# A retention and mixture-of-attention kernel: normalisation ahead of the projections, another order of the start, zero rows under the last tile

## The chip, the cores and the metric

The kernel runs on one core of one Trainium2 chip. Time is device microseconds (us) of one launch. The engines are PE (matmuls; its weight loads are shown apart as PEld), DVE, ACT and POOL (vector work) and SP, which issues the DMAs. Each works through its own instructions in the order in which the program wrote them, and waits on semaphores for the others.

## The reference

Two layers follow one another, for 8 batches, 8 heads, 576 positions and 64 channels per head, all in float32:

```python
# 1: retention, per head with its own decay gamma
scores = scale * (q @ k.T)
ret = scores * where(rel >= 0, gamma ** rel, 0)       # rel = row - column
x = concat over heads of (ret @ v)                    # [B, 576, 512]
# 2: four attention experts of width 64, two chosen per row
logits = x @ w_gate                                   # the two largest of 4, softmax -> w
for e in range(4):
    q, k, v = x @ wq[e], x @ wk[e], x @ wv[e]
    a = softmax(where(causal, scale * q @ k.T, -1e9))
    out += w[e] * (a @ v @ wo[e])                     # w is 0 where e was not chosen
```

## The kernel before, in words

Rows go in tiles of 128, so a batch has five: four of 128 rows and a last one of 64 (the table CH). Tiles 0 and 1 form range 0 (256 rows), tiles 2 to 4 range 1 (320 rows). The program is one loop over n = 0 to 41 and an `end()`; iteration n works on retention tile n (batch n // 5, tile n % 5), finishes retention tile n - 1, takes attention tile n - 6 through scores and softmax, and attention tile n - 7 through transposes and the product with V. So every stage of five iterations repeats for each batch.

The names that the prediction uses, with their tiles:

- `load` brings x (q and k of a tile, transposed) and vk (v and k) through SP's queue. `decay` multiplies v by powers of gamma in place (vk, L102), on DVE for the first four tiles and on POOL from then on (`gp if n > 3 else v`).
- `qk` makes the 64 x 64 products of q and k (qk, L135), copies them out on ACT (p, L138), and POOL masks them (L141). `state` makes k-by-v products (st, L115) and adds them up on DVE (s, L121 and L123).
- `result` is a generator: in its first part q times the earlier state (old, L164), v times the masked products (own, L174), the copies and adds into x32 (x, L167 on ACT, L178 and L179 on DVE); after its first yield the multiply by a table (L184), the rounded high part xh (L185, ACT) and the rest xl (L186). L184 and L186 are on DVE for the first two tiles and on POOL later.
- `proj` (pj, L225) makes attention's q and k, `vproj` (pv, L249) its v and the gate's logits. Each sums three products, high by high, high by low and low by high, since xh, xl and the weights wh, wl are in a reduced float format. `vproj` copies the logits out on DVE (lg, L254 and L256). `weights` splits a weight into high (ACT, L210) and low (DVE, L211).
- `scores` (ss, L315 or L324 for the 64-row tile) with its softmax steps: masked row minimum on DVE (L334, L338), exponential with its sum on ACT (L342). `normal` divides by the sum and multiplies by the gate: three small DVE instructions (L354 to L361) and one pass over each expert's probabilities (L363). `turn` transposes them on PE (pt, L378) and copies the result out on DVE or ACT (L381, L383). `values` multiplies by V (ys, L400). `outproj` (po, L425) writes the result through ACT and SP.

All PE results go through eight PSUM banks of one tag: a new tile takes the bank of the eighth tile before it, and waits until that one's reader is done. Which projections an iteration runs stands in the table STEPS: of batch b, q and k of range 0 in iteration 5b+3, v of range 0 in 5b+5, q and k of range 1 in 5b+6, v of range 1 in 5b+7, output in 5b+9 and 5b+12; batch 0 has its own places. The order of PE, DVE, ACT and POOL is the order of these calls, since the program is scheduled by hand; SP's order is set by the compiler. Within an iteration it is: retention of tile n (`qk`, `state`) interleaved with `result(n - 1)`, `scores` of the new tile with `turn` of the old one between its softmax steps, the second part of `result`, `decay(n + 1)`, the gate, `weights`, the projections (`work(n)`), `normal` of the new tile, `values` of the old one.

In the 64-row tile all blocks are cut to 64 where a column block or a row block ends: `vproj` loads 64 columns, the fifth transpose is 128 x 64, and the fifth step of `values` contracts 64 rows.

## Time and profile before

| | |
|---|---|
| median of three runs | 484.05 us (483.19 to 485.59) |
| the profiled execution's own time | 484.3 us |
| its span | 482.6 us, 19026 instructions |
| granted TensorE clock, mean | 0.982 |
| moved by DMA | 50.98 MB, 106 GB/s in the mean |

A timeline row reads: start and length in us, engine, line, operation, what it writes from what it reads, shape, count, and in brackets idle time of the engine before it and what ended that. For PE the shape begins with rows times columns of the array that are in use (64\*64, 128\*64, 128\*128). Consecutive instructions of one line are merged, so a row's length goes from the first start to the last end; ends of matmuls are modelled, and the start of the next row is the better clock. A row of the wait list reads: who waited for whom, us in total, how often, the longest. A row of the groups by shape: count, busy us in total, mean ns of one, idle time before them.

### The profile page before, as it was taken

The page shows a single profiled execution, that of the slowest core. Times are in us where ns is not written, and L with a number is a line of the kernel's source. Part 1 is how long each engine was busy: PE and PEld are TensorE (multiplying, and loading weights), DVE is VectorE, ACT ScalarE, POOL GpSimd, SP SyncE. Part 2 cuts the span into 40 slices and gives each one's busy share as a digit, 9 for nine tenths or more (in the row PEclk, how much of TensorE's full clock was granted, in tenths as well). Part 3 has the DMA queues.
Part 4 walks back from the last instruction along what each step waited for, and adds up shares of the span by engine and source line. Part 5 has one row for each costly group of instructions (what it writes and reads, how often), then busy time and mean ns, then how long its engine had stood idle before and what let it go on. Part 6 is the DMA issues. An engine that isn't in the chain of part 4 may idle for free.

```text
span 482.6 us, 19026 instructions
## 1 busy us (share of the span) xinstructions
PE 458.3 (95%) x7996; PEld 401.6 (83%) x7996; DVE 314.0 (65%) x1135; ACT 260.0 (54%) x814; POOL 216.0 (45%) x276
## 2 busy tenths in 40 slices
PE   7597999999999999999999999999999999998996
PEld 4486978898789888899888997799788997877785
DVE  2832878663986648864787639866487737793662
ACT  2652667545565455745475455664476455654472
POOL 2247545544465435564355444654446543420100
PEclk8797999999999999999999999999999999999999
DMA  8943322314243142413423142522423110000021
GB/s 288 385 178 134 107 94 88 134 46 144 90 156 111 58 140 89 168 46 103 131 90 133 45 145 90 176 92 75 157 90 133 48 57 1 3 30 16 2 87 67
DMA packets 22516, 50.98 MB, mean 106 GB/s; under 512 B 2720, under 2 KB 11680, under 8 KB 22432
## 3 DMA queue, kind: packets, MB, share of 16 engines
q1 hardware_dynamic: 22432, 49.77, 29.8%
q8 instruction: 63, 1.03, 0.9%
q14 instruction: 21, 0.17, 0.1%
HBM read 40.33 MB, written 9.44 MB: 103 GB/s over the span
## 4 chain that ended last, share of the span: by engine, by line
PE 80%; DVE 9%; ACT 5%; issue 2%; DMA 2%; POOL 1%; SPq 0%; DVEq 0%; ACTq 0%; POOLq 0%
PE pj L225 21%; PE pv L249 11%; PE ys L400 10%; PE po L425 10%; PE pt L378 9%; PE ss L315 5%; PE qk L135 4%; DVE p L363 3%; PE ss L324 3%; PE own L174 2%; PE st L115 2%; PE old L164 2%; DVE x L179 2%; DMA gi<-gi 2%; ACT p L138 1%
## 5 line engine op out<-in xcount | busy, mean ns | idle before, releaser
L342 ACT ACTIVATE p<-p,nm 128x128 f32<-128x128 f32 (+4 forms) x144 | 83.0, 578 | 89.5 <-DVE nm L334 67.4
L186 POOL TENSOR_TENSOR xl<-x,xh 128x512 fp32r<-128x512 f32 (+1 forms) x38 | 44.6, 1174 | 97.3 <-ACT xh L185 97.3
L363 DVE TENSOR_SCALAR p<-p,sm 128x128 f32<-128x128 f32 (+4 forms) x144 | 70.7, 551 | 1.4
L414 POOL CAST yh<-y 128x256 fp32r<-128x256 f32 (+1 forms) x39 | 17.5, 449 | 112.2 <-ACT y L413 112.2
L378 PEld LDWEIGHTS pt<-con,p 128*128 128x128 f32 (+1 forms) x400 | 42.7, 139 | 28.7 <-issue 12.5
L141 POOL TENSOR_SCALAR_AFFINE_SELECT p<-p 64x512 f32<-64x512 f32 (+1 forms) x80 | 49.8, 623 | 30.0 <-ACT p L138 27.2
L334 DVE CUSTOM_DVE_ANT_0 p<-ss,mask 128x512 f32<-128x512 f32 (+3 forms) x128 | 56.2, 482 | 8.5 <-PE ss L315 8.5
L378 PE MATMUL pt<-con,p 128*128 128x128 f32 (+1 forms) x400 | 55.1, 280 | 7.0 <-DVE x L179 3.5
L400 PE MATMUL ys<-pth,vn 128*64 128x128 f32 (+2 forms) x960 | 56.6, 262 | 0.0
L400 PEld LDWEIGHTS ys<-pth,vn 128*64 128x64 f32 (+1 forms) x960 | 46.2, 136 | 8.1 <-issue 3.1
L184 POOL TENSOR_TENSOR x<-x,gi 128x512 f32<-128x512 f32 (+1 forms) x38 | 44.5, 1170 | 13.5 <-PE pt L378 8.7
L254 DVE COPY lg<-pv 128x4 f32<-128x4 f32 (+1 forms) x40 | 6.4, 160 | 66.3 <-ACT vn L253 66.2
L179 DVE TENSOR_TENSOR x<-x,own 128x256 f32<-128x256 f32 (+1 forms) x80 | 26.3, 361 | 35.0 <-ACT x L167 34.7
L315 PE MATMUL ss<-k,q 64*64 64x512 f32 (+3 forms) x512 | 42.6, 432 | 0.5 <-issue 0.5
L381 DVE COPY pth<-pt 128x512 f32<-128x512 f32 (+3 forms) x80 | 37.6, 483 | 4.5 <-PE pt L378 4.2
L102 POOL TENSOR_TENSOR vk<-vk,con 128x512 f32<-128x512 f32 (+1 forms) x36 | 35.3, 980 | 0.0
L383 ACT ACTIVATE pth<-pt 128x512 f32<-128x512 f32 (+3 forms) x80 | 33.1, 420 | 0.5 <-PE pt L378 0.4
L413 ACT ACTIVATE y<-ys 128x256 f32<-128x256 f32 (+1 forms) x39 | 14.1, 363 | 32.7 <-PE ys L400 32.3
L138 ACT ACTIVATE p<-qk 128x256 f32<-128x256 f32 (+1 forms) x80 | 24.6, 359 | 11.3 <-PE qk L135 11.3
L185 ACT ACTIVATE xh<-x 128x512 fp32r<-128x512 f32 (+1 forms) x40 | 23.2, 579 | 11.6 <-POOL x L184 8.0
L253 ACT ACTIVATE vn<-pv 128x256 f32<-128x256 f32 (+1 forms) x40 | 15.1, 381 | 26.5 <-PE pv L249 26.5
L425 PE MATMUL po<-yh,who 128*128 128x320 f32 (+1 forms) x128 | 28.8, 306 | 0.6 <-ACT yh L409 0.6
(89 smaller groups left out, 1038.6 us busy)
## 6 DMA issues: line engine op xcount, KB each, us to landing
x<-xf SPq DMA_DIRECT2D x32, 512.0 KB, 4.3
vk<-vkf SPq DMA_DIRECT2D x32, 512.0 KB, 5.3
out<-ot SPq DMA_DIRECT2D x32, 160.0 KB, 1.9
out<-ot SPq DMA_DIRECT2D x32, 128.0 KB, 1.8
raw<-wraw SPq DMA_DIRECT2D x4, 512.0 KB, 7.0
x<-xt SPq DMA_DIRECT2D x8, 256.0 KB, 2.6
vk<-vkt SPq DMA_DIRECT2D x8, 256.0 KB, 3.2
gi<-gi SPq DMA_DIRECT2D x1, 256.0 KB, 7.6
```

Source lines behind the costliest of these rows:

```text
L141: gp.affine_select(w, w, pattern=[[0, 4 * k], [1, 64]], base=0, channel_multiplier=-1, compare_op=OP.is_ge, fill=0.0)
L184: e.tensor_mul(x32, x32, gi[:, :, t0:t0 + C])
L186: e.tensor_sub(xl[:, :, l0:l0 + C], x32, f(xh[:, :, l0:l0 + C]))
L225: mm(ps, ww[:, kc, p * 128:(p + 1) * 128], xx[:, kc], start=(i == 0), stop=(i == 11))
L249: mm(ps[:C], xx[:, kc, l0:l0 + C], ww[:, kc], start=(i == 0), stop=(i == 11))
L315: mm(ps[2 * p + z][HALF[i]], q[p][HALF[z], l0 + 64 * i:l0 + 64 * i + 64], k[p][HALF[z], :w], start=True, stop=True)
L334: v.tensor_tensor_reduce(p32[:, e], ps[e], mask[:, 512 - w:], -1.0, BIG, OP.add, OP.min, nm[:, e:e + 1])
L342: act(p32[:, e], p32[:, e], AF.Exp, bias=bias, scale=-1.0, accum_out=sm[:, 0, e:e + 1])
L363: v.tensor_scalar(p32[:, e], p32[:, e], rs[:, e:e + 1], None, op0=OP.mult)
L378: nc.tensor.transpose(pt[rows, j - j0], p32[:, e, c0:c0 + jw], ident)
L400: mm(py[64 * z:64 * z + 64, p], VN[b, rr][0][jr, j - 2 * rr, e * D:(e + 1) * D], src, start=(j == 0), stop=(j == t))
L425: mm(ps, ww[:, p, d * 128:(d + 1) * 128], yy[:, p], start=(i == 0), stop=(i == 5))
```

## The change

Four things change.

1. `normal` of the new tile is called ahead of `work(n)` instead of behind it.
2. The range-1 tiles xh and xl become two fixed tiles X1 of 384 columns, whose last 64 columns are set to zero once, on POOL. `vproj` of the last tile then takes 128 columns, the fifth transpose takes a 128 x 128 block of a p32 tile widened to 640 columns (POOL zeroes the last 64 for each last tile), and the fifth step of `values` contracts 128 rows, half of them zero.
3. In the first three iterations `state(n)` comes ahead of the second part of `result(n - 1)`.
4. Of tiles 4 and 5 `decay` is on DVE instead of POOL, the low part of weight q is made on POOL instead of DVE, and weight v is split in iteration 2 instead of 3.

```diff
--- before.py
+++ after.py
@@ -74,6 +74,10 @@
+    X1 = [const.tile([128, 4, 384], F32R, name=f"x1{y}") for y in "hl"]
+    for x in X1:
+        gp.tensor_copy(x[:, :, 320:], mask[:, :256].rearrange("p (k w) -> p k w", k=4))
     HALF = [slice(0, 64), slice(64, 128)]
     X, VK, P, S_, XR = {}, {}, {}, {}, {}
 
@@ -99,7 +103,7 @@
         if 0 < n < 5:
             for kc in range(4):
                 act(gi[:, kc, t0:t0 + C], gi[:, kc, :C], AF.Copy, scale=fac[:, c, kc:kc + 1])
-        (gp if n > 3 else v).tensor_mul(vv, vv, gam[:, 2 * c:2 * c + k].unsqueeze(3).to_broadcast([128, k, 4, D]))
+        (gp if n > 5 else v).tensor_mul(vv, vv, gam[:, 2 * c:2 * c + k].unsqueeze(3).to_broadcast([128, k, 4, D]))
 
     def state(n):
         b, c = divmod(n, 5)
@@ -147,8 +151,7 @@
         q = 0 if c < 2 else 1
         q0, w, tiles = RNG[q]
         if c == tiles[0]:
-            XR[b, q] = (sa.tile([128, 4, w], F32R, name=f"xh{q}", bufs=1),
-                        sa.tile([128, 4, w], F32R, name=f"xl{q}", bufs=1))
+            XR[b, q] = X1 if q else [sa.tile([128, 4, w], F32R, name="x" + y, bufs=1) for y in "hl"]
         xh, xl = XR[b, q]
         old = [bank([128, 2, C], "old") for g in range(2)]
         x, p, vk = X[n], P.pop(n), VK[n]
@@ -208,7 +211,7 @@
         W[n] = (hi, lo)
         for r, cs in [(raw, slice(0, w))] + ([(rg, slice(w, wt))] if n == "v" else []):
             act(hi[:, :, cs], r, AF.Copy)
-            v.tensor_sub(lo[:, :, cs], r, f(hi[:, :, cs]))
+            (gp if n == "q" else v).tensor_sub(lo[:, :, cs], r, f(hi[:, :, cs]))
 
     def proj(b, r, w, p):
         r0, n, tiles = RNG[r]
@@ -222,7 +225,7 @@
         i = 0
         for ww, xx in ((wh, xh), (wh, xl), (wl, xh)):
             for kc in range(4):
-                mm(ps, ww[:, kc, p * 128:(p + 1) * 128], xx[:, kc], start=(i == 0), stop=(i == 11))
+                mm(ps, ww[:, kc, p * 128:(p + 1) * 128], xx[:, kc, :n], start=(i == 0), stop=(i == 11))
                 i += 1
                 if i % 4 == 0 and i < 12:
                     yield
@@ -246,11 +249,11 @@
         i = 0
         for xx, ww in ((xh, W["v"][0]), (xh, W["v"][1]), (xl, W["v"][0])):
             for kc in range(4):
-                mm(ps[:C], xx[:, kc, l0:l0 + C], ww[:, kc], start=(i == 0), stop=(i == 11))
+                mm(ps, xx[:, kc, l0:l0 + 128], ww[:, kc], start=(i == 0), stop=(i == 11))
                 i += 1
                 if i % 4 == 0 and i < 12:
                     yield
-        act(vn[:C, ti], ps[:C, :E * D], AF.Copy)
+        act(vn[:, ti], ps[:, :E * D], AF.Copy)
         v.tensor_copy(lg[:C, ti], ps[:C, E * D:])
         if t == 4:
             v.tensor_copy(lg[64:, ti], ps[:C, E * D:])
@@ -323,7 +326,9 @@
                         j = i ^ z
                         mm(ps[p][j][HALF[z]], q[p][HALF[z], l0:l0 + C], k[p][HALF[z], 288 * j:288 * j + 288],
                            start=True, stop=True)
-        p32 = sb.tile([128, n, w], F32, name="p32", tag="p32", bufs=2)
+        p32 = sb.tile([128, n, w if t < 4 else 640], F32, name="p32", tag="p32", bufs=2)
+        if t == 4:
+            gp.memset(p32[:, :, S:], 0.0)
         sm = sb.tile([128, 2, E], F32, name="sm", tag="sm", bufs=3)
         nm = sb.tile([128, E], F32, name="nm", tag="nm", bufs=3)
         SS[m] = (p32, sm, n)
@@ -339,13 +344,14 @@
                                                -1.0, nm[:, 2 * e:2 * e + 1] if j else BIG, OP.add, OP.min,
                                                nm[:, 2 * e + j:2 * e + j + 1])
                     bias = nm[:, 2 * e + 1:2 * e + 2]
-                act(p32[:, e], p32[:, e], AF.Exp, bias=bias, scale=-1.0, accum_out=sm[:, 0, e:e + 1])
+                act(p32[:, e, :w], p32[:, e, :w], AF.Exp, bias=bias, scale=-1.0, accum_out=sm[:, 0, e:e + 1])
                 yield
 
         return soft()
 
     def normal(m):
         b, t = divmod(m, 5)
+        t0, C = CH[t]
         r = 0 if t < 2 else 1
         ti = t - RNG[r][2][0]
         p32, sm, n = SS[m]
@@ -360,7 +366,7 @@
                 hr = slice(64 * z, 64 * z + 64)
                 v.tensor_mul(rs[hr], rs[hr], wt[hr, ti, z::2])
         for e in range(n):
-            v.tensor_scalar(p32[:, e], p32[:, e], rs[:, e:e + 1], None, op0=OP.mult)
+            v.tensor_scalar(p32[:, e, :t0 + C], p32[:, e, :t0 + C], rs[:, e:e + 1], None, op0=OP.mult)
 
     def turn(m):
         b, t = divmod(m, 5)
@@ -371,16 +377,14 @@
         for e in range(n):
             for j0 in range(0, nj, 4):
                 js = range(j0, min(nj, j0 + 4))
-                rows = slice(0, CH[js[0]][1])
                 pt = bank([128, len(js), 128], "pt")
                 for j in js:
-                    c0, jw = CH[j]
-                    nc.tensor.transpose(pt[rows, j - j0], p32[:, e, c0:c0 + jw], ident)
-                o = pth[rows, e, j0:j0 + len(js)]
+                    nc.tensor.transpose(pt[:, j - j0], p32[:, e, 128 * j:128 * j + 128], ident)
+                o = pth[:, e, j0:j0 + len(js)]
                 if e % 2:
-                    v.tensor_copy(o, pt[rows])
+                    v.tensor_copy(o, pt)
                 else:
-                    act(o, pt[rows], AF.Copy)
+                    act(o, pt, AF.Copy)
                 yield
 
     def values(m):
@@ -392,12 +396,11 @@
         py = bank([128, 2, C], "ys")
         for p in range(2):
             for j in range(t + 1):
-                jr = slice(0, CH[j][1])
                 rr = 0 if j < 2 else 1
                 for z in range(2):
                     e = 2 * p + z
-                    src = pth[jr, e, j] if t < 4 else pth[jr, p, j, 64 * z:64 * z + 64]
-                    mm(py[64 * z:64 * z + 64, p], VN[b, rr][0][jr, j - 2 * rr, e * D:(e + 1) * D], src,
+                    src = pth[:, e, j] if t < 4 else pth[:, p, j, 64 * z:64 * z + 64]
+                    mm(py[64 * z:64 * z + 64, p], VN[b, rr][0][:, j - 2 * rr, e * D:(e + 1) * D], src,
                        start=(j == 0), stop=(j == t))
         if (b, r) not in YU:
             YU[b, r] = (sb.tile([128, 2, n], F32R, name=f"yh{r}", bufs=1),
@@ -514,15 +517,15 @@
         if n < 3:
 
             next(late, None)
-            if n < NC:
-                qk(n)
-                run(late)
+            qk(n)
+            state(n)
+            run(late)
         else:
             if n < NC:
                 qk(n)
             next(late, None)
-        if n < NC:
-            state(n)
+            if n < NC:
+                state(n)
         soft = scores(new[0]) if new else iter(())
         turns = (None for m in old for _ in turn(m))
         for i, _ in enumerate(soft):
@@ -532,13 +535,13 @@
         decay(n + 1)
         run(turns)
         gates()
-        for w in {1: "kq", 3: "v", 6: "o"}.get(n, ""):
+        for w in {1: "kq", 2: "v", 6: "o"}.get(n, ""):
             weights(w)
         for m in new[1:]:
             run(scores(m))
-        run(work(n))
         for m in new:
             normal(m)
+        run(work(n))
         for m in old:
             values(m)
     end()
```

The first place is DVE between the last softmax step of an iteration with v of range 1 and the next iteration's softmax (iterations 17 to 18; p is the probabilities' tile). Before:

```order
L381 COPY pth<-pt 128x128
L334 ISA p_3125,nm<-ss,mask 128x256
L334 ISA nm 128x1
L381 COPY pth<-pt 128x128
L254 COPY lg<-pv 128x4 x2
L254 COPY lg<-pv 64x4
L256 COPY lg<-pv 64x4
L354 TENSOR_SCALAR sm<-sm 128x4
L355 RECIPROCAL sm<-sm 128x4
L357 TENSOR_TENSOR sm<-sm,wt 128x4
L363 TENSOR_SCALAR p_3125<-p_3125,sm 128x256 x4
L179 TENSOR_TENSOR x_3290<-x_3290,own 128x2x128 x2
```

Changed (line numbers are 3 to 6 higher):

```order
L385 COPY pth<-pt 128x128
L339 ISA p_3125,nm<-ss,mask 128x256
L339 ISA nm 128x1
L385 COPY pth<-pt 128x128
L360 TENSOR_SCALAR sm<-sm 128x4
L361 RECIPROCAL sm<-sm 128x4
L363 TENSOR_TENSOR sm<-sm,wt 128x4
L369 TENSOR_SCALAR p_3125<-p_3125,sm 128x256 x4
L257 COPY lg<-pv 128x4 x2
L257 COPY lg<-pv 64x4
L259 COPY lg<-pv 64x4
L182 TENSOR_TENSOR x_3288<-x_3288,own 128x2x128 x2
```

The three small steps and the four passes of the normalisation stand ahead of the gate copies, which read pv, instead of behind them.

The second place is DVE in iterations 1 to 3, from the first x adds on. Before:

```order
L184 TENSOR_TENSOR x_179<-x_179,gi 128x512
L186 TENSOR_TENSOR xl_176<-x_179,xh_175 128x4x128
L123 TENSOR_TENSOR s<-st,s 128x128 x4
L102 TENSOR_TENSOR vk<-vk,con 128x2x256
L211 TENSOR_TENSOR wlk<-raw,whk 128x1024
L211 TENSOR_TENSOR wlq<-raw,whq 128x1024
L179 TENSOR_TENSOR x_281<-x_281,own 128x2x128 x2
L184 TENSOR_TENSOR x_281<-x_281,gi 128x512
L186 TENSOR_TENSOR xl_176<-x_281,xh_175 128x4x128
L123 TENSOR_TENSOR s<-st,s 128x128 x4
L102 TENSOR_TENSOR vk<-vk,con 128x2x256
```

Changed:

```order
L127 TENSOR_TENSOR s<-st,s 128x128 x4
L187 TENSOR_TENSOR x_183<-x_183,gi 128x512
L189 TENSOR_TENSOR xl<-x_183,xh 128x4x128
L106 TENSOR_TENSOR vk<-vk,con 128x2x256
L214 TENSOR_TENSOR wlk<-raw,whk 128x1024
L182 TENSOR_TENSOR x_285<-x_285,own 128x2x128 x2
L127 TENSOR_TENSOR s<-st,s 128x128 x4
L187 TENSOR_TENSOR x_285<-x_285,gi 128x512
L189 TENSOR_TENSOR xl<-x_285,xh 128x4x128
L106 TENSOR_TENSOR vk<-vk,con 128x2x256
L214 TENSOR_TENSOR wlv<-raw,whv 128x4x256
L214 TENSOR_TENSOR wlv<-rg,whv 128x4x4
```

The state adds stand ahead of each multiply, wlq is no longer there, and wlv has come up from behind the third tile's adds.

## The prediction

> **What bounds the kernel now.** I read the page's head first, then the table of stretches, then the list of who waited for whom on PE, then the timelines of PE, DVE, ACT and POOL at the places which that list names.
>
> ```profile
> PE 458.3 (95%) x7996; PEld 401.6 (83%) x7996; DVE 314.0 (65%) x1135; ACT 260.0 (54%) x814; POOL 216.0 (45%) x276
> ```
>
> ```profile
> 12.00:24.00 12.00, 6.26 (x155) 5.68 (x148) 9.99 (x21) 7.48 (x21) 3.11 (x4) 0.78 1.03 385
> 36.00:48.00 12.00, 9.12 (x242) 8.32 (x242) 2.58 (x12) 3.58 (x12) 8.60 (x10) 0.72 0.37 134
> 48.00:480.00 432.00, 422.83 (x7176) 371.89 (x7175) 294.98 (x1085) 239.77 (x756) 196.50 (x247) 1.00 0.27 90
> ```
>
> The columns are stretch, length, then busy time of PE, PEld, DVE, ACT and POOL, granted clock, DMA share, GB/s. PE is the bound: 95% over all, 98% after 48 us at clock 1.00. Its holes are a start of 48 us with the clock at 0.72 to 0.78, and small repeated waits:
>
> ```profile
> PE pt L378 <- DVE x L179: 3.5, 7, 0.6
> PE st L115 <- POOL vk L102: 2.9, 1, 2.9
> PE pt L378 <- DVE s L123: 1.7, 7, 0.2
> ```
>
> Two rows occur seven times, once per batch, at the transposes of the 256-wide tile (iterations 8, 13, ... 38; the timeline shows 18). One of them on the timeline, PE:
>
> ```profile
> 178.69 1.50 PE L315 MATMUL ss<-k,q 64*64 64x384 f32 x16
> 180.71 0.77 PE L378 MATMUL pt<-con,p 128*128 128x128 f32 x4 [0.52 <-DVE x L179]
> 181.73 0.63 PE L378 MATMUL pt<-con,p 128*128 128x128 f32 x4 [0.25 <-DVE s L123]
> 182.31 0.74 PE L225 MATMUL pj<-xh,whk 128*128 128x256 f32 x4
> ```
>
> The same passage where nothing waits (another iteration):
>
> ```profile
> 143.24 2.12 PE L324 MATMUL ss<-k,q 64*64 64x288 f32 x16
> 145.29 1.97 PE L378 MATMUL pt<-con,p 128*128 128x128 f32 x16
> 147.01 0.73 PE L249 MATMUL pv<-whv,xh 128*128 128x260 f32 x4
> ```
>
> There the transposes start 0.07 us before the scores' modelled end and run at (147.01-145.29)/16 = 0.1075 us each. By that pace the eight at 180.71 would start at 180.12 and the projection at 180.98, not 182.31. So the stall costs 1.33 us, more than the 0.77 us of idle time in brackets: delay inside a modelled matmul isn't idle. What is late is DVE:
>
> ```profile
> 173.83 0.16 DVE L254 COPY lg<-pv 128x4 f32<-128x4 f32 x1 [4.42 <-ACT vn L253]
> 177.77 2.55 DVE L363 TENSOR_SCALAR p<-p,sm 128x256 f32<-128x256 f32 x4
> 180.25 0.74 DVE L179 TENSOR_TENSOR x<-x,own 128x256 f32<-128x256 f32 x2
> 180.91 0.87 DVE L123 TENSOR_TENSOR s<-st,s 128x128 f32<-128x128 f32 x4
> 181.71 0.54 DVE L334 CUSTOM_DVE_ANT_0 p<-ss,mask 128x384 f32<-128x384 f32 x1
> ```
>
> DVE idles 4.42 us for the first gate copy (L254), stays behind pv until the last copy, and then normalises for 2.55 us when PE is already in the next iteration; x, s and the masked row minimum (L334) queue behind that. The eight PSUM banks go round in the order of allocation, so the four pt tiles of this iteration get the banks of own (freed by L179) and of st (freed by L123), and the projection gets the first ss bank (freed by L334, at 182.25). PE waits for each of the three in turn.
>
> **Normalisation in front.** Only where the iteration's projections are pv does DVE's order change, since kq and po put nothing on DVE; this part leaves the orders of ACT and PE as they are. normal() needs the exponentials' sums; ACT is done with them early, and the next iteration's x on DVE needs this ACT copy:
>
> ```profile
> 170.07 0.19 ACT L342 ACTIVATION_READ_ACCUMULATOR p<-p,nm 128x1 f32 x1
> 178.04 0.67 ACT L167 ACTIVATE x<-old 128x256 f32<-128x256 f32 x2
> ```
>
> So it runs from 170.26 for 0.72 (three small ones, 177.05 to 177.77) plus 2.55, to 173.5, before the first gate copy at 173.83. The 3.3 us hide under pv; without that cover we have today's state. The gate copies follow at about the times they have now; what they free, a pv bank, is asked for again only eight allocations later, in the next iteration. Late next is x: L167 ends 178.71, x runs to 179.45, s to 180.32, L334 to 180.86; the banks are free at 179.5 and 180.3 for transposes due at 180.12 and 180.55, the projection's at 180.86 for 180.98. The whole 1.33 goes: 7 x 1.33 = **9.3 us**. Bounds: 7 x 0 if a bank still comes late, 7 x 1.40 at the best pace; the value stands near the upper end since each bank is met with 0.1 to 0.6 us. In the other pv iteration (143 to 152 us) no PE wait follows, gain 0. In iteration 39 the same move starts DVE's run earlier, which ends in the single 1.18 us wait here:
>
> ```profile
> 435.21 0.64 PE L378 MATMUL pt<-con,p 128*128 128x128 f32 x2 [1.18 <-DVE nm L334]
> ```
>
> There the normalisation starts at 420.6, after two gate copies, though its sums are there at 419.0, and DVE then works without a break to the L334 which frees the bank. Starting 1.6 earlier it meets two things that don't move: the 64-row scores (its first L338 goes from 424.3 to about 423.2) and PE's transposes, whose last copy can't begin before about 426. I take **0.75 us** of the 1.18 (0 to 1.18).
>
> **Zero rows.** In values() of a batch's last tile the fifth block has 64 rows:
>
> ```profile
> 443.37 0.69 PE L400 MATMUL ys<-pth,vn 128*64 128x64 f32 x16
> 470.32 0.33 PE L400 MATMUL ys<-pth,vn 64*64 64x64 f32 x4
> 469.71 1.82 PE L400 MATMUL ys<-pth,vn 128*64 128x64 f32 x40
> 471.48 1.67 PE L378 MATMUL pt<-con,p 128*128 128x128 f32 x12
> ```
>
> Sixteen of 128 rows start within 0.69-0.228 (the mean of one in its group) = 0.46, so 0.031 each. Forty, with four changes of row count, take 471.48-469.71 = 1.77; at one step they take 1.24. That is 0.53 for the last two batches. In the other six, 64-row qk matmuls follow, so the change on leaving stays (162.46 to 163.98 now, 1.52; then 39 x 0.031 + about 0.17 = 1.38): 0.14 each. Sum 2 x 0.53 + 6 x 0.14 = **1.9 us** (bounds 0 and 3). What changes the width, not the rows, costs nothing:
>
> ```profile
> 154.18 1.31 PE L378 MATMUL pt<-con,p 128*128 128x128 f32 x10
> 155.24 0.83 PE L225 MATMUL pj<-xh,whk 128*128 128x320 f32 x4
> 174.18 0.64 PE L249 MATMUL pv<-whv,xl 128*128 128x260 f32 x4
> 174.66 0.64 PE L249 MATMUL pv<-whv,xh 128*64 128x260 f32 x4
> 175.13 0.64 PE L249 MATMUL pv<-wlv,xh 128*64 128x260 f32 x4
> ```
>
> The last tile's ten transposes, two of them 64 wide, take (155.24-154.18)/10 = 0.106 each, no more than the full ones above, and four pv take 0.48 in either width. So the padding of both is worth 0. [...] The weight loads of pv's padded tile do get longer:
>
> ```profile
> L249 PEld LDWEIGHTS pv<-whv,xh 128*128 128x128 f32 x128 | 18.1, 193 | 1.1 <-ACT k L230 0.9
> L249 PEld LDWEIGHTS pv<-whv,xh 128*64 128x64 f32 x32 | 3.9, 134 | 0.0
> ```
>
> They run beside the matmuls, which keep their pace in both widths; if that cover were gone, 8 x 12 x 0.059 = 5.7 us. POOL gets eight memsets of 128 elements per partition (a 224-wide one at the start took 0.28) ahead of the 64-row tile's multiply. Behind it the multiply, the subtraction and the next vk shift by that much, and the subtraction idles 2.2 us for ACT there: hidden. The wider copies out of PSUM cover more partitions, not more elements in a row: 0.
>
> **The head.** DVE, then PE:
>
> ```profile
> 13.12 1.05 DVE L184 TENSOR_TENSOR x<-x,gi 128x512 f32<-128x512 f32 x1
> 15.54 0.87 DVE L123 TENSOR_TENSOR s<-st,s 128x128 f32<-128x128 f32 x4
> 18.18 1.22 DVE L211 TENSOR_TENSOR wlq<-raw,whq 128x1024 fp32r<-128x1024 f32 x1
> 21.95 0.73 PE L225 MATMUL pj<-xh,whk 128*128 128x256 f32 x4 [2.83 <-ACT xh L185]
> 35.25 0.74 PE L249 MATMUL pv<-wlv,xh 128*128 128x260 f32 x4 [0.43 <-DVE wlv L211]
> 40.47 1.14 PE L115 MATMUL st<-vk 64*64 64x64 f32 x32 [2.88 <-POOL vk L102]
> 46.62 0.72 PE L115 MATMUL st<-vk 64*64 64x64 f32 x32
> ```
>
> State adds in front free old's second half 2.4 us earlier (15.54 becomes 13.1), but nothing after it ends earlier: the first projection waits for two L184 multiplies in a row, and each now has 0.87 of state adds before it. The first delays ACT's run (xh, tables, whk, whq, x) by 0.8; the second comes on top; wlq's 1.22 leave DVE. Net +0.8, projection at 22.75. wlq on POOL waits for whq and runs, at twice to three times the 1.04 of the 512-wide vk, to 21.5 or so; the select behind it is needed by own at about 28.4, and the last four projections need wlq at 27. The two casts that zero the shared tiles run on POOL before its first select at 7.55. Then weights v: its two ACT copies and two DVE subtractions move under the first 24 projections, where ACT and DVE idle over 3 us each, so the 0.43 goes, and an ACT wait of 0.74 before the first pv with it. The first pv then ends 0.75 ahead instead of 0.8 behind. Of iterations 4 and 5 the vk decay moves to DVE, which idles 2.4 us there; the st matmul at 40.47 finds its vk at about 36.7, ready to start. The pv behind it waits for a bank until about 38.2 (ACT's copy of p, behind xh, behind POOL's multiply). Late next is POOL: its run of select, multiply, subtraction and vk decay between 36 and 45 us loses one decay (1.04) and starts about 0.9 earlier, since ACT is free sooner; waits for ACT inside it shrink a little too. By the durations it has now, its vk for the st at 46.62 comes at about 43.5. So the head ends **3.1 us** earlier. Bounds: 2.0, if the 0.8 isn't recovered, and 5.5, if that last wait vanishes and st stands right behind own. The raw o weights' fetch on SP moves behind one tile's two loads; its user comes at 51 us.
>
> **Sum.** Against the profiled execution (span 482.6, its own time 484.3; the median of the runs shown is 484.05, 0.05% lower): 9.3 + 0.75 + 1.9 + 3.1 = 15.05, so 469.3; on the median's base 469.0. I forecast **469**.
>
> **Rivals.**
> 1. The seven stalls turn into bank waits: DVE's work stretches beside POOL's (a 256-wide L363 takes 0.64 here, while the 384-wide ones, by shape, take 0.42 in the mean), so x, s or L334 come late in the new place. Half the gain: 469+4.7 = 473.7, at the limit 478. Against it: 0.1 us and more in hand. 14%.
> 2. The head gives nothing: PE idles 4.7 instead of 2.8 us before 22.75, and the clock, 0.72 to 0.78 after idling, stays low. 472. 14%.
> 3. The head gives all 5.5: a busier PE keeps the clock that fell to 0.72 in 36 to 48. 466.5. 12%.
> 4. PE pays for the padding: the 5.7 us of weight loads come to light and the 1.9 are gone, 476.6. Against: the equal 0.48 above. 5%.
> 5. Slower: from 48 us on PE has no pauses left, and the granted clock falls under the load. PE's 423 us grow by the inverse of the clock; at 0.965 the 15 us are used up, and at 0.95 (+22) it ends at 491. Against: 1.00 through 432 us with PE 98% busy; low clock goes with idleness here. 3%. [...]
> 6. [...] 3%.
>
> My forecast holds 49% (467 to 471.5). **Range** 465 to 475: it takes in 2, 3 and most of 1, and leaves out 4, 5, 6 and the tail of 1, where the seven stalls stay whole. A difference under 0.5% (2.4 us) can't be told from no change here; only 5 and a failure of several terms come near it: faster 0.95, same 0.03, slower 0.02.
>
> **What would show it.** Right: PE's list no longer has its two rows with seven waits; DVE's normalisation lies before the gate copies; from scores to projection in those iterations 2.3 instead of 3.6 us; forty ys in 1.24; the first projection near 22.8, the 46.62 st near 43.5, held by POOL. Wrong: pt waiting for x, s or nm seven times again; pv at over 0.12 per matmul; a clock under 1.00 after 48 us.

## The result, and the profile after

| | before | after |
|---|---|---|
| median, same chip | 483.62 us (482.73 to 485.59, 4 runs) | 471.92 us (470.27 to 473.67, 4 runs) |
| the profiled execution's own time | 484.3 us | 470.27 us |
| its span | 482.6 us | 468.5 us |
| granted clock, mean | 0.982 | 0.985 |

The ratio is 0.9758, with a 95% interval of 0.9731 to 0.9785: 11.7 us by the medians, 14.0 between the two profiled executions. The forecast was 469.0, range 465 to 475. The profiled execution of the changed kernel is the quickest of its four, so the comparison of the two traces flatters the change by about 2 us; where the difference lies is shown below.

The list of waits on PE after the change (who waited for whom; us in total, times, the longest):

```profile
PE pj L228 <- ACT xh L188: 4.2, 1, 4.2
PE st L119 <- POOL vk L106: 1.6, 1, 1.6
...
PE st L119 <- DVE lg L257: 1.6, 1, 1.6
...
PE pt L382 <- DVE nm L339: 1.2, 1, 1.2
```

No row with seven waits is left. What is left are single waits: most of them in the start, the old one for nm and a few short ones in the end, and, below these rows, a new one of `own` for `lg` (0.4). The table of stretches (length, then busy time of PE, PEld, DVE, ACT and POOL, granted clock, DMA share, GB/s):

```profile
36.00:48.00 12.00, 8.81 (x256) 8.17 (x249) 5.57 (x31) 5.57 (x23) 9.04 (x10) 1.00 0.56 194
48.00:466.00 418.00, 414.33 (x7158) 368.78 (x7156) 301.51 (x1066) 237.72 (x747) 196.52 (x254) 1.00 0.27 92
```

PE is busy for 99% of the long stretch (98% before). The clock stays at 1.00 there, and between 36 and 48 us it is 1.00 where it was 0.72.

**The seven passages.** PE's timeline at the place that the prediction showed (scores, transposes, projection of an iteration):

```profile
172.22 0.48 PE L318 MATMUL ss<-k,q 64*64 64x384 f32 x1
...
172.25 1.50 PE L318 MATMUL ss<-k,q 64*64 64x384 f32 x15
173.68 1.09 PE L382 MATMUL pt<-con,p 128*128 128x128 f32 x8
174.53 0.72 PE L228 MATMUL pj<-xh,whk 128*128 128x256 f32 x4
```

DVE's timeline there:

```profile
165.28 2.70 DVE L369 TENSOR_SCALAR p<-p,sm 128x256 f32<-128x256 f32 x3
167.91 0.15 DVE L257 COPY lg<-pv 128x4 f32<-128x4 f32 x1
...
172.32 0.75 DVE L182 TENSOR_TENSOR x<-x,own 128x256 f32<-128x256 f32 x2 [1.77 <-ACT x L170]
```

The normalisation (L369) now lies before the first gate copy, and DVE idles 1.77 us before the x add. The eight transposes go in one row. From the first score to the projection it is 174.53 - 172.22 = 2.31 us (3.62 before). Against the trace of before each of six passages is 1.24 to 1.34 us shorter; the first (iteration 8) only 0.69.

**Where 14.0 us went**, by comparing the starts of the same PE groups in both traces:

| term | predicted | measured, trace against trace |
|---|---|---|
| start (to the first q and k projection of range 1) | 3.1 | 2.7 (47.71 to 45.00) |
| seven passages | 9.3 | 8.5 |
| single wait in the end | 0.75 | -0.5 |
| zero rows | 1.9 | 2.1 |
| two gaps of PE that the profile calls "issue" | not foreseen | 1.2 |
| sum | 15.05 | 14.0 |

### The profile page after: what moved, and what is told of

It reads as the page before. It is cut to its first block, busy times and chain, and to the rows that moved or that the text cites. A ratio compares the mean times of both kernels' runs of the same rounds, so it can differ in the third digit from the quotient of the medians.

```text
span 468.5 us, 19045 instructions
## 1 busy us (share of the span) xinstructions
PE 450.1 (96%) x7996; PEld 398.9 (85%) x7996; DVE 323.8 (69%) x1136; ACT 260.0 (55%) x814; POOL 219.1 (47%) x285
## 4 chain that ended last, share of the span: by engine, by line
PE 88%; DVE 3%; ACT 3%; POOL 2%; DMA 2%; issue 1%; SPq 0%; ACTq 0%; POOLq 0%; DVEq 0%
PE pj L228 22%; PE po L428 11%; PE pv L252 11%; PE pt L382 10%; PE ys L403 10%; PE ss L318 8%; PE qk L139 4%; PE ss L327 3%; PE own L177 3%; PE st L119 3%; PE old L167 3%; DMA gi<-gi 2%; POOL x L187 1%; DVE p L369 1%; ACT gi L105 1%
## 5 line engine op out<-in xcount | busy, mean ns | idle before, releaser
L369 DVE TENSOR_SCALAR p<-p,sm 128x128 f32<-128x128 f32 (+4 forms) x144 | 78.9, 607 | 1.4
L382 PEld LDWEIGHTS pt<-con,p 128*128 128x128 f32 x400 | 43.1, 141 | 20.5 <-issue 12.0
L189 POOL TENSOR_TENSOR x1l<-x,x1h 128x512 fp32r<-128x512 f32 (+1 forms) x24 | 26.6, 1106 | 62.8 <-ACT x1h L188 62.8
L382 PE MATMUL pt<-con,p 128*128 128x128 f32 x400 | 52.8, 278 | 1.6 <-DVE nm L339 1.2
L403 PE MATMUL ys<-pth,vn 128*64 128x128 f32 (+1 forms) x960 | 53.0, 260 | 0.0
L403 PEld LDWEIGHTS ys<-pth,vn 128*64 128x64 f32 x960 | 44.3, 137 | 5.9 <-issue 1.5
L187 POOL TENSOR_TENSOR x<-x,gi 128x512 f32<-128x512 f32 (+1 forms) x38 | 44.7, 1177 | 4.1 <-DVE x L182 0.5
L106 POOL TENSOR_TENSOR vk<-vk,con 128x512 f32<-128x512 f32 (+1 forms) x34 | 34.0, 1000 | 0.0
L189 POOL TENSOR_TENSOR xl<-x,xh 128x512 fp32r<-128x512 f32 x14 | 18.8, 1342 | 31.5 <-ACT xh L188 31.5
L256 ACT ACTIVATE vn<-pv 128x256 f32<-128x256 f32 x40 | 15.1, 383 | 24.8 <-PE pv L252 24.8
L177 PE MATMUL own<-p,vk 64*64 64x64 f32 x1152 | 26.7, 223 | 2.0 <-issue 1.6
```

Of the source, the lines that this page charges most:

```text
L187: e.tensor_mul(x32, x32, gi[:, :, t0:t0 + C])
L189: e.tensor_sub(xl[:, :, l0:l0 + C], x32, f(xh[:, :, l0:l0 + C]))
L369: v.tensor_scalar(p32[:, e, :t0 + C], p32[:, e, :t0 + C], rs[:, e:e + 1], None, op0=OP.mult)
L382: nc.tensor.transpose(pt[:, j - j0], p32[:, e, 128 * j:128 * j + 128], ident)
L403: mm(py[64 * z:64 * z + 64, p], VN[b, rr][0][:, j - 2 * rr, e * D:(e + 1) * D], src, start=(j == 0), stop=(j == t))
```

## The experiments

All times are medians; "before" was run on the same chip each time (483.91, 482.56 and 484.66 us for the three groups of kernels). The changed kernel was run again in the last group: 471.38 us (470.69 to 472.04). None of the kernels leaves work out.

### The normalisation alone, and the change without it

The changed kernel with `normal` behind the projections again:

```diff
-        for m in new:
-            normal(m)
         run(work(n))
+        for m in new:
+            normal(m)
```

> The changed kernel with normal() behind work(n) again, all else as changed. Theory (DVE's normalisation behind the gate copies makes the seven stalls, and nothing else in the change touches them): the two rows with seven waits of pt for DVE x and s are back, and the seven passages from scores to projection grow by about 1.3 us each (6 x 1.31 + 0.72 as the changed kernel's trace lost), the 0.5 us stall at the scores of iteration 40 goes; about +8 us, 478 to 479 on a profile of 470.3. Rival (the stalls went because the head, POOL's lighter load or the padding made x, s or the banks earlier): under 3 us more, no seven waits.

Measured: 480.22 us (479.99 to 480.38), ratio to before 0.9918 (0.9897 to 0.9939). Its waits on PE:

```profile
PE pt L382 <- DVE x L182: 3.5, 7, 0.5
...
PE pt L382 <- DVE s L127: 1.8, 7, 0.3
```

Both rows with seven waits are back, almost as in the kernel before (3.5 and 1.7). Group by group, six passages are 1.31 to 1.35 us longer than in the changed kernel and that of iteration 8 is 0.69 longer: 8.7 us. The scores of iteration 40 come 0.52 sooner; the rest of the difference is a later start in that execution.

The kernel before with only this edit:

```diff
+        for m in new:
+            normal(m)
         run(work(n))
-        for m in new:
-            normal(m)
```

> The kernel before with only normal() moved ahead of work(n). Theory: -8 us, about 476 against 484, the seven waits gone, a new 0.6 us wait of own in iteration 8 and of 0.5 at the scores of iteration 40, both for gate copies that now stand behind the normalisation. Rival (it needs the other parts to show): less than 4 us.

Measured: 475.2 us (474.8 to 476.02), ratio 0.9815 (0.9795 to 0.9836). Its passage:

```profile
178.06 1.09 PE L378 MATMUL pt<-con,p 128*128 128x128 f32 x8
178.91 0.71 PE L225 MATMUL pj<-xh,whk 128*128 128x256 f32 x4
```

The transposes run without a wait, as in the changed kernel. Against the trace of before: the seven passages -8.55, the scores of iteration 40 +0.50. So this edit does the same with and without the others: 8.5 us of gain and 0.5 of loss. By the medians it is 8.3 us in one direction (480.22 to 471.92) and 8.7 in the other (483.91 to 475.2). Settled.

### The zero rows, and the widths without them

The changed kernel with all of the padding taken out (64 columns in `vproj`, 64-wide fifth transposes, no memset, 64 rows in the fifth step of `values`):

```diff
-                mm(ps, xx[:, kc, l0:l0 + 128], ww[:, kc], start=(i == 0), stop=(i == 11))
+                mm(ps[:C], xx[:, kc, l0:l0 + C], ww[:, kc], start=(i == 0), stop=(i == 11))
...
-                    nc.tensor.transpose(pt[:, j - j0], p32[:, e, 128 * j:128 * j + 128], ident)
+                    nc.tensor.transpose(pt[rows, j - j0], p32[:, e, c0:c0 + jw], ident)
```

> The changed kernel without zero rows: the last tile's v projection, fifth transpose and fifth values step cut to 64 again, no memsets. Theory (only the row count of the values step costs): forty ys take 1.6 instead of 1.16 us from first to last, +0.29 per batch for six batches and +0.59 for one, in all +2.3 us, 472.6. [...] Rival B (wider weight loads cost): faster than the changed kernel.

Measured: 473.31 us (473.11 to 473.48), ratio 0.9774 (0.9756 to 0.9791).

Only the values step cut back to 64 rows; `vproj` and the transposes keep their full width:

```diff
+                jr = slice(0, CH[j][1])
...
-                    mm(py[64 * z:64 * z + 64, p], VN[b, rr][0][:, j - 2 * rr, e * D:(e + 1) * D], src,
+                    mm(py[64 * z:64 * z + 64, p], VN[b, rr][0][jr, j - 2 * rr, e * D:(e + 1) * D], src,
```

> The changed kernel with the v projection and the fifth transpose padded to 128 columns, but the fifth values step on 64 rows. Theory (rows cost, widths don't): the same time as with no padding at all, +2.3 us against the changed kernel. [...] Rival B (wider weight loads cost up to 5.7 us): slower than the unpadded one.

Measured: 473.45 us (473.09 to 474.52), ratio 0.9781 (0.9759 to 0.9802). The forty values matmuls on PE's timeline, this kernel:

```profile
157.63 1.77 PE L404 MATMUL ys<-pth,vn 128*64 128x64 f32 x38
159.15 0.27 PE L139 MATMUL qk<-x 64*64 64x64 f32 x2
159.23 0.22 PE L404 MATMUL ys<-pth,vn 64*64 64x64 f32 x2
```

and the changed kernel, whose forty are of one kind:

```profile
156.86 1.39 PE L403 MATMUL ys<-pth,vn 128*64 128x64 f32 x40
158.18 0.69 PE L139 MATMUL qk<-x 64*64 64x64 f32 x32
```

By the medians both kernels are 1.4 to 1.5 us slower than the changed one (471.92), but the intervals of the ratios overlap with its own, so the size rests on the traces. These agree at every batch: 0.29 us is lost after the forty matmuls where 64-row products follow, 0.59 in the last batch but one, nothing at pv or at the transposes. So all of the gain hangs on the rows in `values`. The widths bring nothing, and the longer weight loads of the padded pv (188 ns here, 134 ns for 64 columns in the kernel before) cost nothing. That kills the rival that PE pays for the padding, and no cost of the width itself is seen. (0.29 is half of 0.59 and twice the 0.14 that the prediction had for those batches.)

### The start

The start of the changed kernel as it was before, with the other changes kept: `state` behind `result`'s second part, decay of tiles 4 and 5 on POOL, the low part of weight q on DVE, weight v in iteration 3.

```diff
-        (gp if n > 5 else v).tensor_mul(vv, vv, gam[:, 2 * c:2 * c + k].unsqueeze(3).to_broadcast([128, k, 4, D]))
+        (gp if n > 3 else v).tensor_mul(vv, vv, gam[:, 2 * c:2 * c + k].unsqueeze(3).to_broadcast([128, k, 4, D]))
...
-            (gp if n == "q" else v).tensor_sub(lo[:, :, cs], r, f(hi[:, :, cs]))
+            v.tensor_sub(lo[:, :, cs], r, f(hi[:, :, cs]))
...
-            state(n)
             run(late)
+            state(n)
...
-        for w in {1: "kq", 2: "v", 6: "o"}.get(n, ""):
+        for w in {1: "kq", 3: "v", 6: "o"}.get(n, ""):
```

> The changed kernel with the start as before: state behind the second part of result, decay of tiles 4 and 5 on POOL, low part of q on DVE, weight v split in iteration 3. Theory: the 2.7 us of the head come back and nothing else moves: first projection at 22.0 instead of 22.9, the first kq1 projection at 47.7 instead of 45.0; +2.7, 473. Rival (the start's order sets the clock of the whole start, so it is worth more): +4 or more. Rival (the start was worth nothing of its own): under 1.

Measured: 473.41 us (472.26 to 475.33), ratio 0.9804 (0.9767 to 0.984). PE in this kernel:

```profile
40.12 0.69 PE L119 MATMUL st<-vk 64*64 64x64 f32 x32 [2.83 <-POOL vk L106]
...
45.59 0.84 PE L228 MATMUL pj<-x1h,whk 128*128 128x320 f32 x4
```

The old wait of 2.8 us at 40 us is back, and yet the range-1 projection starts at 45.59, only 0.59 later than in the changed kernel (45.00). In the trace of before the same st started at 40.47 and the projection at 47.71. The difference between these two lies behind the wait: there the twelve pv matmuls took 2.55 us from the first start to the last, here they take 1.42; the clock in 36 to 48 us was 0.72 there and is 1.00 here.

The 0.59 is not yet what the old start costs, because the first loads of an execution come sooner or later by chance (the two executions of the changed kernel differ by 0.67 there), and here they came soon. A common point is the first tile's last x add on DVE, which the program has ahead of all these edits: it starts at 12.10 here, at 13.17 in the changed kernel, at 12.80 in the trace of before, and between 12.10 and 13.82 over all fourteen profiled executions. From it to the range-1 projection are 33.49 us here, 31.83 in the changed kernel (31.83 to 32.99 in the six executions with the same start) and 34.91 before. So against the changed kernel's profiled execution the old start costs 1.7 us when the clock survives the pause (0.5 against the slowest of the six), and 3.1 when it does not. The clearest part is the stretch from the qk products behind the first projections to the range-1 projection: 17.33 us in the changed kernel, 19.17 here, 20.96 before. Of these 3.6 us, 1.8 stay when the clock is 1.00, and 1.8 come with the clock at 0.72.

The four runs of this kernel spread by 3 us: 472.26 and 472.61 at a mean clock of 0.985 and 0.989, 474.22 and 475.33 at 0.975 (which of their stretches was cold, that is at a clock under 1.00, the mean does not tell; in the profiled one, 472.61, a stretch near 424 us was cold too, see the last section). The theory's fixed 2.7 is wrong: it mixes waits and clock. Between 36 and 48 us the clock was 1.00 in all eleven profiled executions that have the decay of tiles 4 and 5 on DVE, and 0.72, 0.86 and 1.00 in the three with the old start; that the shorter pauses (1.56 and 1.63 below, for 2.88) are the reason is made likely by this, but not shown.

What the new start does to PE, in the changed kernel (PE, then DVE, then POOL):

```profile
36.85 0.25 PE L119 MATMUL st<-vk 64*64 64x64 f32 x2
38.66 0.68 PE L119 MATMUL st<-vk 64*64 64x64 f32 x28 [1.56 <-DVE lg L257]
39.27 0.75 PE L252 MATMUL pv<-whv,xh 128*128 128x260 f32 x4
...
43.94 0.69 PE L119 MATMUL st<-vk 64*64 64x64 f32 x32 [1.63 <-POOL vk L106]
```

```profile
38.44 0.16 DVE L257 COPY lg<-pv 128x4 f32<-128x4 f32 x1 [2.10 <-ACT vn L256]
```

```profile
42.83 1.05 POOL L106 TENSOR_TENSOR vk<-vk,con 128x512 f32<-128x512 f32 x1
```

vk of that st comes early now and a PSUM bank is late in its place (1.56 us, freed by the logits copy); the st after it waits for POOL's vk as predicted.

**The order of the state adds.** The changed kernel with `state(n)` behind `result`'s second part:

```diff
-            state(n)
             run(late)
+            state(n)
```

> The changed kernel with only state() behind the second part of result again in the first three iterations. Theory (two times 0.87 us of state adds stand ahead of the two multiplies for which the first projection waits): first projection at 21.2 instead of 22.9, kq1's start about 1 us earlier than 45.0, so -1 us, 469. Rival (old's second half, which waits for these adds, comes 2.3 us later and holds up ACT's copy of x and all behind it): first projection not earlier than 22.9, +0 to +2 us.

Measured: 471.69 us (469.94 to 473.05), ratio 0.9762 (0.9727 to 0.9797): no difference. PE's first projection in this kernel, and the first instruction behind it:

```profile
22.15 1.22 PE L228 MATMUL pj<-xh,whk 128*128 128x256 f32 x4 [2.67 <-ACT xh L188]
...
25.93 1.05 PE L228 MATMUL pj<-xl,whq 128*128 128x256 f32 x4
26.79 0.97 PE L228 MATMUL pj<-xh,wlq 128*128 128x256 f32 x4
27.69 0.52 PE L139 MATMUL qk<-x 64*64 64x64 f32 x20
```

and in the changed kernel:

```profile
22.89 1.23 PE L228 MATMUL pj<-xh,whk 128*128 128x256 f32 x4 [4.16 <-ACT xh L188]
...
26.64 0.64 PE L228 MATMUL pj<-xl,whq 128*128 128x256 f32 x4
27.11 0.63 PE L228 MATMUL pj<-xh,wlq 128*128 128x256 f32 x4
27.67 0.52 PE L139 MATMUL qk<-x 64*64 64x64 f32 x20
```

The projection starts 0.74 earlier and ends at the same time: what it gains it spends at half the pace, since PE is cold for longer (granted clock in 26 to 28 us 0.62, in the changed kernel 0.86; four matmuls every 0.86 us to the end, where the changed kernel takes 0.47 from 26.64 on). The 0.74 is not chance of the loads: the first tile's last x add starts at 13.15 here and at 13.17 there (the changed kernel's second execution has the projection at 22.22, but its x add at 12.50). From that add to the start of the second tile's xh on ACT the chain takes 9.04 us in both executions of the changed kernel, 8.47 in the kernel before and 8.32 here. So the state adds cost 0.6 to 0.7 us on that chain (0.8 predicted), and nothing at its end in this execution. The expected 1.7 did not come, because the second tile's table multiply (L187) took 1.72 us here, where POOL makes the low part of weight q during most of it, and 1.04 in the changed kernel, where it does not.

**One more decay off POOL**, that of tile 6:

```diff
-        (gp if n > 5 else v).tensor_mul(vv, vv, gam[:, 2 * c:2 * c + k].unsqueeze(3).to_broadcast([128, k, 4, D]))
+        (gp if n > 6 else v).tensor_mul(vv, vv, gam[:, 2 * c:2 * c + k].unsqueeze(3).to_broadcast([128, k, 4, D]))
```

> The changed kernel with the vk decay of tile 6 on DVE as well. Theory (POOL's run of select, multiply and subtraction is what the st at 43.94 waits for, 1.63 us): that wait goes and st stands right behind own; -1.7 us, 468.6. Rival (another wait ends at the same place, own for POOL's select or a bank): under 0.5 us gained.

Measured: 471.27 us (470.07 to 471.89), ratio 0.9747 (0.9715 to 0.978).

```profile
43.16 0.62 PE L119 MATMUL st<-vk 64*64 64x64 f32 x26 [0.51 <-DVE lg L257]
```

The wait for POOL's vk (1.63) is gone, and a bank that DVE's logits copy frees takes its place with 0.51. From the qk products behind the first projections to the range-1 projection it is 16.31 us instead of 17.33, so the edit gives 1.0 of the expected 1.7. The projection itself starts at 44.21, 0.79 earlier, because the first tile's last x add came 0.24 later in this execution. The median does not show it.

**Nine warm-up matmuls** ahead of the first projection, on a tile of zeros that the program already has:

```diff
         for m in new:
             normal(m)
+        if n == 2:
+            warm(9)
         run(work(n))
```

> The changed kernel with nine more warm-up matmuls (results unused) on PE right ahead of the first projections, where it idles 4.2 us. Theory (the first 24 projections take 4.6 instead of 2.8 us only because the clock has fallen while PE idled): they take 2.8 to 3.0, and all that follows moves up by about 1.7 us; 468.6, and the spread of the runs shrinks, since it comes from the clock of the start. Rival (the projections are slow for another reason, weights or xl coming late): they still take 4.6 and nothing is gained, or the warm-up delays them.

Measured: 470.19 us (469.21 to 472.87), ratio 0.9742 (0.9703 to 0.9781).

```profile
19.81 3.00 PE L69 MATMUL pw<-wz 128*128 128x512 bf16 x9
23.32 0.73 PE L228 MATMUL pj<-xh,whk 128*128 128x256 f32 x4 [0.51 <-ACT xh L188]
...
26.96 0.69 PE L139 MATMUL qk<-x 64*64 64x64 f32 x32
...
44.29 0.86 PE L228 MATMUL pj<-x1h,whk 128*128 128x320 f32 x4
```

The first four matmuls now take 0.73 instead of 1.23, the 24 of the projection 3.44 instead of 4.58 (granted clock in 24 to 36 us 1.00 instead of 0.89), so 1.1 of the expected 1.7 is there. PE is at the range-1 projection only 0.71 earlier, because the first projection began 0.43 later in this execution (23.32 for 22.89), of which 0.23 was there at the first tile's last x add already. Nothing is lost behind it: from the qk products at 26.96 to the range-1 projection it is 17.33 us, as in the changed kernel, and st still waits 1.48 for POOL's vk.

### The end, and all together

The changed kernel with `normal` behind the projections in iteration 39 alone:

```diff
-        for m in new:
-            normal(m)
+        if n != NC - 1:
+            for m in new:
+                normal(m)
         run(work(n))
+        if n == NC - 1:
+            for m in new:
+                normal(m)
```

> The changed kernel with normal() behind the projections in iteration 39 alone. If the gate's logits copy behind the normalisation is what holds the scores of iteration 40 (they wait 0.52 us for a pv bank which that copy frees), the 0.52 goes and the end comes 0.5 us earlier, unless the transposes' wait for DVE nm in the end (1.2 us) grows by as much as the work that moves behind. If the scores wait for something else: no difference in their step, total as the changed kernel.

Measured: 471.67 us (470.36 to 472.44), ratio 0.9737 (0.9704 to 0.9771), against 471.38 of the changed kernel on the same chip: no difference that these runs can tell. In the traces it does what was expected. The changed kernel (PE, then DVE):

```profile
407.81 2.65 PE L327 MATMUL ss<-k,q 64*64 64x288 f32 x16
```

```profile
405.49 2.69 DVE L369 TENSOR_SCALAR p<-p,sm 128x512 f32<-128x512 f32 x4
408.11 0.22 DVE L257 COPY lg<-pv 128x4 f32<-128x4 f32 x2
```

This kernel:

```profile
408.26 2.13 PE L327 MATMUL ss<-k,q 64*64 64x288 f32 x16
```

The sixteen scores take 0.52 less, since the logits copies no longer stand behind the normalisation; 0.14 of that is given back at the transposes' wait in the end (3.67 to 3.81 us from the first to the projection behind them).

> The changed kernel once more, beside the next three. Both theories expect its median near 471.9 us, with runs between 470 and 474 by the clock that the start gets.

That was the changed kernel: 471.38 us, as expected. Then four edits together, each as in its diff above: state adds behind, decay of tile 6 on DVE, nine warm-ups, normalisation behind in iteration 39.

> The changed kernel with four edits: state() behind result's second part as in the kernel before, decay of tile 6 on DVE, nine warm-up matmuls ahead of the first projection, normal() behind the projections in iteration 39. If the gains measured one by one add up (0.0, 0.8, 0.7, 0.5): 2.0 us under the changed kernel, 470.0. If the first two gain from the same wait at the start (PE held at 44 us by the vector work) and not from each other: 0.8 to 1.2 under it, 470.9.

Measured: 468.41 us (467.95 to 470.48, 6 runs), ratio 0.968 (0.9648 to 0.9712): 3.0 us under the changed kernel on the same chip, and in this group all its runs lie under all of the changed kernel's. PE behind the first projections, and at the range-1 projection:

```profile
25.91 0.69 PE L139 MATMUL qk<-x 64*64 64x64 f32 x32
...
42.21 0.85 PE L228 MATMUL pj<-x1h,whk 128*128 128x320 f32 x4
```

The range-1 projection starts 2.8 earlier than in the changed kernel, where the edits one by one gave 0.8, 0.7 and 0.0. That looks like more than the sum, but the traces do not show that the edits help each other. The stretch between the two rows is 16.31 us, as with the decay of tile 6 alone, and the 24 first projections take 3.42, as with the warm-ups alone (3.44). What differs is the chance of the loads: the first tile's last x add is 0.50 sooner than in the changed kernel here, and was 0.24 and 0.23 later with the two edits alone. From that add on, the range-1 projection comes 2.3 sooner with all edits, and 1.0, 0.9 and 0.0 sooner with one at a time.

The medians' 3.0 is not all the edits' either. The two profiled executions of this group are 3.0 us apart as well, but 1.5 of it is a clock that fell near 424 us in the changed kernel's (last section). The mean clock of five of the six runs is 0.993 here, where the changed kernel's six have 0.978 to 0.989; how much of that is the warm start and how much is luck near 424 us was not measured.

The same without the first edit:

> The same four edits but for the first: state() stays ahead as in the changed kernel. The warm-up matmuls raise the clock early but the first projection then waits for the table multiplies, 0.8 us later than with state() behind. If the start is bound by vector work till 44 us, as the first projection that came 0.7 earlier with nothing gained at the end says, this is the same as with state() behind within 0.3 us; if with a warm clock PE is the bound there, this is 0.7 us slower.

Measured: 469.01 us (467.55 to 472.6), ratio 0.9695 (0.9657 to 0.9733). In the traces the first projection starts at 22.99 instead of 22.28 and the range-1 projection at 42.89 instead of 42.21. That is the 0.7 of the second theory, but 0.6 of it is there at the first tile's last x add already (13.27 for 12.67), ahead of the edit: from that add on, the two kernels differ by 0.1. The medians differ by 0.6 in the same direction, and the runs overlap. What `state` behind is worth with a warm clock stays open.

## Why the prediction was right or wrong

**Right: normalisation ahead.** The mechanism (three banks late because DVE normalises in PE's next iteration) and its size hold: 1.24 to 1.34 per passage for 1.33 predicted, in six of seven, and both directions of the experiment agree.

**Wrong: "the gate copies follow at about the times they have now; what they free, a pv bank, is asked for again only eight allocations later".** This holds where the normalisation ends well before the projections do. It fails at two places. In iteration 8 of the changed kernel (DVE, then PE):

```profile
59.06 3.10 DVE L369 TENSOR_SCALAR p<-p,sm 128x256 f32<-128x256 f32 x4
62.09 0.28 DVE L257 COPY lg<-pv 128x4 f32<-128x4 f32 x3
```

```profile
62.38 0.75 PE L177 MATMUL own<-p,vk 64*64 64x64 f32 x30 [0.38 <-DVE lg L257]
```

The first batch has no earlier output to project, so the iteration is shorter, the normalisation ends when pv is already done, and three logits copies in one row free their banks too late: own waits, and 0.6 of the 1.33 is lost. The second place is iteration 40, where only the last tile's 32 short products of `old` and `own` stand between the projections' end and the scores: 0.52, which the experiment on iteration 39 gives back. I had looked for who waits for x, s and L334, and not at the one instruction that the normalisation was moved past.

**Wrong in sign: the single wait in the end** (0.75 predicted, -0.5 measured). The loss is the 0.52 just named. The wait for nm itself did not shrink (PE, then DVE):

```profile
421.58 0.64 PE L382 MATMUL pt<-con,p 128*128 128x128 f32 x2 [1.20 <-DVE nm L339]
```

```profile
420.31 0.42 DVE L339 CUSTOM_DVE_ANT_0 p<-ss,mask 128x256 f32<-128x256 f32 x1 [0.47 <-PE pt L382]
```

"DVE then works without a break" was the step that failed: DVE is ahead now and idles 0.47 us until PE's transposes let it go on, so an earlier start of DVE cannot move the end of this wait. Which of the tiles ties the two together was not tried.

**Right with a term off: zero rows** (1.9 predicted, 2.1 measured). Rows cost and widths do not, as forecast, and the copies over more partitions do not either (vn on ACT takes 383 ns over 128 partitions, and took 377 over 64). The gain on leaving was mis-sized: 0.29 per batch in place of 0.14. On the last tile of all the forty matmuls got shorter, but the time went into a new wait of the transposes behind them (PE):

```profile
455.52 1.44 PE L403 MATMUL ys<-pth,vn 128*64 128x64 f32 x40
457.29 1.84 PE L382 MATMUL pt<-con,p 128*128 128x128 f32 x12 [0.33 <-DVE p L369]
```

So of "2 x 0.53" only one came (0.59), and 0.17 of the other's end was lost on top.

**The start** (3.1 predicted, 2.7 in the trace). The steps came nearly as written: first projection at 22.89 (22.75), st behind own held by POOL until 43.94 (43.5), the wait for a bank until 38.66, with pv behind it at 39.27 (38.2; it is st that waits, and for a logits copy instead of p's copy, on the same chain of POOL's multiply and ACT's xh). But the reason for its size is in part another: from the first tile's last x add on, the old start is 3.1 us slower in the trace of before, and 0.5 to 1.7 with a clock that stays up. That the first figure equals the forecast is luck. The step that was wrong is the pricing by waits alone, with the clock only as a rival in both directions; in the trace of before, the wait of 2.88 and the matmuls behind it, with a mean clock of 0.72 in 36 to 48 us, belong to one account.

**The rivals.** That the stalls become bank waits came true in one of seven passages, and in the end. That the head gives nothing or everything: neither. Padding paid by weight loads: ruled out by the two padding experiments. That a change of width costs PE time as one of rows does: no run shows it; without any padding the kernel took 473.31 us, with the widths alone padded 473.45. A clock that falls under load: 1.00 for 418 us in the profiled execution. The sign that the prediction gave for it, a clock under 1.00 after 48 us, did appear in the second execution (0.60 near 424 us), but behind short waits.

The sum came near for partly wrong reasons: 15.05 predicted, 14.0 between the traces, of which 1.2 are gaps that chance put into the one trace and not the other, and 11.7 by the medians. The median of 471.92 lies in the range, but just outside the 467 to 471.5 that the prediction held most likely, and beside rival 2's 472, though the start did give its share.

## What to carry to other kernels

When work is moved ahead of a wait on an in-order engine, list what stands behind it now, however small, and follow each such instruction to the bank it frees, in the shortest iteration (the first batch, the drain at the end) as well as in the usual one. Price a start of short stalls together with the clock that follows them: here the same stretch was 1.8 us shorter without the old waits, and 3.6 where the clock had fallen behind them. Compare starts from an instruction ahead of all edits: the first loads came up to 1.7 us sooner in one execution than in another, which hid part of what single edits gave and made four together look like more than their sum. Pad the contraction rows of a few odd matmuls among many full ones, if zeros are cheap to make (here 0.21 us of POOL a batch, for a gain of 0.29 on PE, 0.59 in the last batch but one); padding their widths brought nothing here.

## What the runs showed of the hardware that was not expected

**The clock fell in the middle of the run after short waits.** The changed kernel's second execution, table of stretches:

```profile
418.00:422.00 4.00, 2.80 (x31) 1.94 (x29) 3.45 (x18) 2.32 (x10) 1.21 (x2) 1.00 0.39 131
422.00:426.00 4.00, 3.65 (x15) 3.45 (x15) 2.82 (x11) 2.02 (x9) 0.00 (x0) 0.60 0.00 0
```

After the wait for nm in the end (1.2 us at most at a time, PE busy for 2.8 of 4 us) the clock was 0.60 for one stretch, and the 48 projection matmuls there took 8.51 us instead of 6.97. This happened in 4 of the 14 profiled executions, with the same waits at that place (3.67 us from the first transpose to the projection in these four, 3.56 to 3.83 in the others), so the length of the waits does not decide it; what does is open. It makes up most of the difference between the changed kernel's two profiled executions, with spans of 468.5 and 470.3. In the start it was low as well: 0.50 from 20 to 26 us, where PE did nothing in the first 2, in both executions of the changed kernel and in the one with `state` behind; then 0.86, 0.79 and 0.62 until 28, and the 24 first projections took 4.58, 5.00 and 5.27 us.

**Gaps at fixed places of PE's instruction stream.** In 7 executions of 14 PE stops behind its 1980th matmul (once behind the next one), and in some behind its 2985th or close to it, for nothing that the profile can name. The kernel with all four edits:

```profile
104.05 1.09 PE L318 MATMUL ss<-k,q 64*64 64x256 f32 x15 [0.94 <-issue]
```

The gap is at the same count, 4033 or 4034 instructions of PE with the weight loads and the waits for semaphores, in the kernel before (at 110 us) and in kernels with nine more matmuls ahead of it, so in these traces it goes with the count and not with the work. The two places are about 6081 - 4033 = 2048 instructions apart. Where the gap occurs, two starts lie 0.6 to 1.3 us apart; in the other seven executions the widest pair there is 0.2 to 0.5. What makes PE stop there was not shown; no run tested it. Both gaps were in the trace of before and neither in that of after, which is 1.2 us of their difference.

**The moved pass got slower.** The changed kernel's groups of instructions by shape (count, busy us, mean ns of one, idle us before them):

```profile
L369 DVE TENSOR_SCALAR p<-p,sm 128x256 f32<-128x256 f32 x32 | 22.0, 750 | 0.3
```

The same pass took 650 ns before; that over 576 columns went from 517 to 794, that over 384 stayed (418 and 423). The place alone does it: in the kernel before with only `normal` moved they are 750 and 794, in the changed kernel with `normal` behind again 651 and 518. The 32 passes over 256 columns cost 3.2 us more of DVE's time, and nothing at the end but in iteration 8, where the last of them ends too late. It is slow beside work on POOL: in the changed kernel the 22 passes over 256 columns with POOL busy for more than half of them took 934 ns in the mean, the other ten 345; before it was 813 for 21 and 339 for eleven. Over 576 columns six took 1266 and ten 511, where before all sixteen lay beside no such work. No run moved POOL's work away, so this is read from the traces alone.
